# A memory-recurrent attention mixer with a gated MLP: GpSimd's left-over products wait for the second half's normalised scores, four half-tiles of MLP work change their step, and the last full projection moves ahead of three left-over groups

## The chip, the core and the metric

One core of a Trainium2 chip runs the whole kernel. Its engines are PE (TensorE, matrix products), DVE (VectorE), ACT (ScalarE), POOL (GpSimd) and SP (SyncE, which issues most transfers). The metric is the device time of one execution in microseconds. The kernel before takes 747.86 us in the median of 3 runs (747.28 to 749.27).

## The reference

The input `x` is 2048 rows of 512 numbers. Two branches read it and a gate mixes them:

```python
g = _sigmoid((x * gate_w).sum(-1, keepdims=True))
a = _A_ref(x, A_mem0, A_Wq, A_Wk, A_Wv, A_Wo, A_seg_len)
b = _B_ref(x, B_w1, B_b1, B_w2, B_b2)      # layernorm, 512 -> 1376, gelu, 1376 -> 512
return g * a + (1 - g) * b
```

Branch A is a recurrence over 64 segments of 32 rows. Each segment is joined to a memory of 8 rows, goes through attention with 32 heads of 128, and the first 8 rows of the result are the next segment's memory:

```python
for s in range(n_seg):
    h = jnp.concatenate([mem, xs], axis=1)           # 8 + 32 rows
    q, k, v = (jnp.einsum('btd,dhe->bhte', h, W) for W in (Wq, Wk, Wv))
    p = _softmax(jnp.where(mask, q @ k^T * scale, -1e9))
    o = jnp.einsum('bhte,hed->btd', p @ v, Wo)
    mem = o[:, :M, :]
```

## The kernel before, in words

The first 70 us run most of the MLP: the hidden layer of all 16 row tiles, and the second layer of seven of them. The hidden layers of the nine others (`DEF`, tiles 1, 3, 5, ...) go to DRAM and come back later. Then 63 steps, one a segment, do the recurrence, and an ending does segment 63. Instructions run on each engine in the order in which the code issues them (`tc.manual_schedule`), so the code is the schedule. `T, si = divmod(s, 4)` names the row tile and the segment in it.

A step has 40 rows, which do not fit the 32-row groups of PE. So 32 rows, 24 of the segment and the 8 of the memory, go through the step itself (`hT`), and the 8 left-over rows of each of four segments are projected together, a tile ahead, as "side" work (`left_qk`, `left_v`). On PE a step runs: queries and keys (L129), scores of the first half of the heads (`scores(s, 0)`), the values (L148), scores of the second half, the products with the values (`av`, L291 and L296, first half and then second), the output projection of the step before (`wo_pass`, L160, 32 matrix products of 512 columns into a bank `X`), and three transposing products that make the next memory (`new_mem`, L761, called with n = 0, 1, 2), whose casts (L763 on DVE) the next step's queries wait for. `run(n)` between these parts takes n pieces of side work.

What touches the change:

- **Normalising.** For the memory's queries the weights must be normalised before `av`. `mnorm(0)` does the first half of the heads and `mnorm(1)` the second: a reciprocal (L824) and a product on DVE that overwrites columns of `E` (L825, in the trace `E<-E,SbF` and `E<-E,RS`). The second half of `av` reads what `E<-E,RS` wrote. The 32 other queries are normalised a step later: DVE makes their reciprocals (L727, `R`), SP sends them to DRAM and back spread over all partitions (`r_dr`, then `Rb`), and GpSimd multiplies. That is `x_norm(s - 1)`, issued at the head of step s: two products into `UT` (L745, 128x384, for this step's `wo_pass`) and two into `UL` (128x128, the left-over rows, for `wo_left`, the side work of the next tile's step si = 2). Behind them GpSimd adds `R` into `racc` (L737), copies left-over queries (L250) and the next step's rows (L246). `Rb` has one buffer, so the next load of it waits for the last product that reads it.
- **Deferred MLP.** `mlp_halves` does the second layer of the nine deferred tiles in halves: one half is 4 matrix products of 256 columns into the bank `W` (L689), two halves use up one tile `hm` of the hidden layer, 11 of these a row tile. `next(mlp)` does one half. `hm_load` on SP fetches, once a step, in `recip_x`, as many tiles as were used up since (`owed`), into 5 buffers; step 2 also fetches four in one piece (`c`). After the eleventh, `mlp_out` writes the result (DVE `ct<-W`, 128x512, then a transfer). In step 2 the side work is `mlp_units(8)`: one unit is two halves.
- **Ending.** Segment 63 makes no memory. After its sums PE does three groups of `wo_left` (`run(3)`, 12 products from `UL`), then the `wo_pass` of segment 62, then `av`. `UL`'s last 8 columns are cleared by GpSimd just before (L896), behind the products of `x_norm(62)`.

## Time and profile before

| what | value |
|---|---|
| time, median of 3 runs (lowest to highest) | 747.86 us (747.28 to 749.27) |
| the profiled execution | 750.09 us, of which 748.2 us are the span from first to last instruction |
| PE busy | 732.8 us, 98% of the span |
| ACT, DVE, POOL busy | 536.7, 448.9 and 246.6 us |
| mean granted TensorE clock | 0.997 |

A step takes a little over 10 us, so step s = 31 lies at about 400 to 411 us. "Busy" of PE counts a product from its start to a modelled end; products overlap, so their starts tell more. A row of a timeline reads: start in us, us, engine, line, operation, output<-inputs, shape, count, and in brackets the idle time before it and what ended that. Several rows of one kind that follow each other are merged. In a row of a wait there stand the total, how many times, and the longest.

### The profile page before, as it was taken

Reading aid. Unit: us, or ns where it says so; the run is one execution under the profiler, and the core shown is the slowest. Engines: PE = TensorE matmul, PEld = TensorE weight load, DVE = VectorE, ACT = ScalarE, POOL = GpSimd, SP = SyncE. Lnnn points to the kernel's source line nnn. Section 1 sums busy time; section 2 is a strip of 40 time slices with the busy share of each in tenths; the row PEclk is TensorE's granted clock in tenths of the full one; section 3 lists DMA queues with packets and bytes.
Section 4 is the critical chain, followed back from the end, with each engine's and each line's share of the span. In section 5 each row is a group of like instructions: output and inputs, shape, how many; then the busy total and the mean of one; then the engine's idle time right before and its main releaser. Section 6 shows DMA issues by size and latency. Waiting matters only on the chain. (4 is left out here: it accounts for less than half of the span.)

```text
span 748.2 us, 44010 instructions
## 1 busy us (share of the span) xinstructions
PE 732.8 (98%) x19147; PEld 428.8 (57%) x19147; DVE 448.9 (60%) x1541; ACT 536.7 (72%) x1629; POOL 246.6 (33%) x515
## 2 busy tenths in 40 slices
PE   8999998999999999999999999999999999999997
PEld 5776554556565555555555555555555555555553
DVE  6877554656565555656565665556665656555554
ACT  6777765777777777777777777777777777777664
POOL 4001332332334333343234334243333343333331
PEclk9999999999999999999999999999999999999999
DMA  8999222222222323122321323231322313222221
GB/s 308 343 360 360 84 83 55 69 87 80 78 68 62 97 74 93 47 83 80 93 79 38 96 75 97 69 81 57 92 78 82 85 44 94 69 90 70 85 63 61
DMA packets 61944, 76.82 MB, mean 103 GB/s; under 512 B 26729, under 2 KB 51922, under 8 KB 60210
## 3 DMA queue, kind: packets, MB, share of 16 engines
q1 hardware_dynamic: 60802, 72.51, 31.1%
q8 instruction: 151, 2.47, 1.3%
q0 software_dynamic: 400, 0.92, 0.3%
q10 hardware_dynamic: 544, 0.52, 0.2%
q14 instruction: 47, 0.39, 0.2%
HBM read 60.21 MB, written 7.70 MB: 91 GB/s over the span
## 5 line engine op out<-in xcount | busy, mean ns | idle before, releaser
L134 ACT CAST Tb<-U 128x512 bf16<-128x512 f32 x288 | 168.8, 586 | 82.5 <-PE U L129 76.8
L745 POOL TENSOR_TENSOR UT<-XR,Rb 128x384 bf16<-128x384 bf16 x126 | 114.1, 927 | 324.6 <-DMA Rb<-r_dr 228.0
L129 PEld LDWEIGHTS <-hT 128*32 128x32 bf16 x4096 | 108.8, 97 | 97.8 <-issue 2.0
L129 PE MATMUL U<-Wq_sb,hT 128*32 128x512 bf16 x2048 | 145.9, 382 | 0.4 <-DVE hT L763 0.4
L129 PE MATMUL U<-Wk_sb,hT 128*32 128x512 bf16 x2048 | 145.2, 381 | 0.0
L148 PE MATMUL X<-Wv_sb,hT 128*32 128x512 bf16 x2048 | 142.9, 378 | 0.0
L160 PE MATMUL X<-Wo_sb,UT 128*32 128x512 bf16 x2016 | 120.8, 380 | 0.0
L834 ACT CAST V<-X 128x256 bf16<-128x256 f32 x256 | 88.7, 372 | 16.0 <-PE X L148 1.1
L138 DVE STREAM_TRANSPOSE QT<-Tb 128x256 f32<-128x256 f32 x128 | 57.0, 445 | 71.1 <-ACT Tb L134 70.9
L763 DVE CAST hT<-U 128x8 bf16<-128x8 f32 x126 | 20.8, 167 | 130.9 <-PE U L761 96.6
L160 PEld LDWEIGHTS <-UT 128*32 128x32 bf16 x2048 | 56.4, 96 | 55.7 <-issue 16.6
L721 ACT CAST XR<-U 128x256 bf16<-128x256 f32 x252 | 78.6, 438 | 0.0
L752 ACT CAST w<-X 128x128 bf16<-128x128 f32 x189 | 44.8, 310 | 41.7 <-PE X L160 41.0
L138 DVE STREAM_TRANSPOSE KT<-Tb 128x256 f32<-128x256 f32 x128 | 57.0, 445 | 25.9 <-ACT Tb L134 25.9
L737 POOL TENSOR_TENSOR racc<-racc,R 128x128 f32<-128x128 f32 x63 | 28.8, 457 | 105.7 <-DVE R L735 101.1
L148 PEld LDWEIGHTS <-hT 128*32 128x32 bf16 x2048 | 45.2, 95 | 20.6
L689 PE MATMUL W<-w_sb,hm 128*32 128x256 bf16 x728 | 50.5, 273 | 3.6 <-DMA hm<-h_dr 3.6
L865 ACT CAST UT<-U 128x64 bf16<-128x64 f32 x252 | 35.4, 227 | 25.9 <-PE U L296 25.9
L745 POOL TENSOR_TENSOR UL<-XR,Rb 128x128 bf16<-128x128 bf16 x126 | 51.5, 430 | 0.0
L809 ACT ACTIVATE E<-U 128x64 bf16<-128x64 f32 (+1 forms) x128 | 35.0, 273 | 9.3 <-PE U L271 0.4
L484 PEld LDWEIGHTS <-w_sb 128*128 128x128 bf16 (+1 forms) x352 | 34.1, 100 | 10.4
L160 PE MATMUL X<-Wo_sb,UL 128*32 128x512 bf16 x512 | 38.7, 379 | 1.0 <-POOL UL L896 1.0
(184 smaller groups left out, 1250.5 us busy)
## 6 DMA issues: line engine op xcount, KB each, us to landing
Rb<-r_dr SPq DMA_DIRECT2D x63, 512.0 KB, 3.9
Wv_sb<-in_A_Wv_dram SPq DMA_DIRECT2D x4, 1024.0 KB, 7.5
Wq_sb<-in_A_Wq_dram SPq DMA_DIRECT2D x4, 1024.0 KB, 8.5
Wk_sb<-in_A_Wk_dram SPq DMA_DIRECT2D x4, 1024.0 KB, 8.4
Wo_sb<-in_A_Wo_dram SPq DMA_DIRECT2D x4, 1024.0 KB, 12.6
VP<-VL SPq DMA_DIRECT2D x64, 64.0 KB, 3.7
hm<-h_dr SPq DMA_DIRECT2D x91, 32.0 KB, 2.6
c<-c_dr SPq DMA_DIRECT2D x16, 128.0 KB, 4.6
```

The source lines that it names most:

```text
L129: nc.tensor.matmul(bk[32 * j:32 * j + 32, :], lhsT=G[:, kc, :], rhs=W5[t][:, kc, h0:h1, j, :], start=(kc == 0), stop=(kc == KC - 1), tile_ ...
L134: nc.scalar.copy(out=Tb[:], in_=bk.rearrange("p (a b e) -> p a e b", a=8, b=2))
L138: nc.vector.transpose(out=dst[:, 8 * hf:8 * hf + 8, c0:c0 + 32, :].rearrange("p a r b -> p a (r b)").bitcast(FP32), in_=Tb[:].rearrange("p ...
L148: nc.tensor.matmul(bk[32 * j:32 * j + 32, :], lhsT=G[:, kc, :], rhs=Wv5[:, kc, 4 * vb:4 * vb + 4, j, :], start=(kc == 0), stop=(kc == KC - ...
L160: nc.tensor.matmul(bk[32 * c:32 * c + 32, :], lhsT=U_[:, j, i, :], rhs=Wo_sb[:, 4 * i + j, :], start=(n == 0), stop=(n == NW - 1), tile_po ...
L689: nc.tensor.matmul(W[32 * c:32 * c + 32, cc], lhsT=hm[:, 32 * c:32 * c + 32], rhs=w2_sb[:, fc, cc], start=(fc == 0 and h == 0), stop=(fc = ...
L721: nc.scalar.copy(out=XR[:, j], in_=U[j][:, 0:NG * 40].rearrange("p (i q) -> p i q", q=40)[:, :, 0:32])
L745: nc.gpsimd.tensor_tensor(out=out[:, :, 4 * h:4 * h + 4, o:o + b - a], in0=XR[:, :, 4 * h:4 * h + 4, a:b], in1=Rb[:, h, :, :, r:r + b - a] ...
L752: nc.scalar.copy(out=w[:, a:b], in_=bk[:, a:b])
L809: nc.scalar.activation(out=E[:, 4 * i2:4 * i2 + 4, c], in_=Sb[i2][:, :, c], func=ACTF.Exp, scale=scale)
L834: nc.scalar.copy(out=V[:, i0:i0 + 2, :].rearrange("p i e -> p (i e)"), in_=(X1, X2)[vb][:, 256 * h:256 * h + 256])
L865: nc.scalar.copy(out=UT[s % 2][:, j, :, 0:M], in_=U[j][:, 0:NG * 40].rearrange("p (i q) -> p i q", q=40)[:, :, 32:40])
```

## The change

Four edits, one of them in two places:

- `x_norm` takes a second argument: 0 makes the `UT` products, 1 the `UL` products. The first is still issued at the head of the step. The second is issued behind the value casts, after a new GpSimd copy of one column of `E` into a new tile `pend`. That copy reads a column that `mnorm(1)` writes, so GpSimd waits for it there. Only in the last segment do both stay at the head.
- `mlp_units(8)` of step 2 becomes `mlp_units(6)`: four halves fewer there. One half more is done at the end of step 3, three at the end of step 4.
- In the ending, `run(3)` comes behind `wo_pass` and not ahead of the reciprocal.

```diff
@@ side() @@
-            gens = [wo_left(T - 1, X1) if T >= 1 else mlp_units(8)]
+            gens = [wo_left(T - 1, X1) if T >= 1 else mlp_units(6)]
@@ x_norm @@
-    def x_norm(s):
+    def x_norm(s, l):
         T, si = divmod(s, SPT)
-        XR, Rb = XRs.pop(s), Rbs.pop(s)[:].rearrange("p (c j) (h q) -> p h j c q", c=4, h=2)
-        for out, o, a, b, r in ((UT[(s + 1) % 2], M, LEFT, 32, 0), (UL[T % 2], LEFT * si, 0, LEFT, 32 - LEFT)):
-            for h in range(2):
-                nc.gpsimd.tensor_tensor(...)
+        XR, Rb = XRs[s], Rbs[s][:].rearrange("p (c j) (h q) -> p h j c q", c=4, h=2)
+        out, o, a, b, r = ((UT[(s + 1) % 2], M, LEFT, 32, 0), (UL[T % 2], LEFT * si, 0, LEFT, 32 - LEFT))[l]
+        for h in range(2):
+            nc.gpsimd.tensor_tensor(...)
@@ head of a step @@
-            x_norm(s - 1)
+            x_norm(s - 1, 0)
+            if last:
+                x_norm(s - 1, 1)
@@ behind the value casts @@
+        if s:
+            nc.gpsimd.tensor_copy(out=pend[:], in_=E[:, NG - 1, 55:56])
+            x_norm(s - 1, 1)
         run(W1)
@@ end of a step @@
         for _ in fill:
             pass
+        for _ in range({SPT - 1: 1, SPT: 3}.get(s, 0)):
+            next(mlp, None)
+            mlp_outs()
@@ ending @@
     fill = wo_left(T, X2)
-    run(3)
     nc.vector.reciprocal(out=R[:, nx], in_=SbF[:, 0:32 * NG])
     nc.scalar.activation(out=rmin[:, nx], in_=R[:, nx], func=ACTF.Copy, accum_out=tot[:, 3:4])
     ws[s - 1] = wo_pass(UT[s % 2])
+    run(3)
```

In what follows, numbers behind a name tell buffers apart, and lines of the kernel after are a few higher (L865 is the copy into `pend`).

GpSimd, one step in the middle, before (what each row waits for stands in brackets):

```order
L246 COPY hT_86<-xT 128x4x24
L745 TENSOR_TENSOR UT_1372<-XR,Rb 128x4x4x24 [waits DMAHW3_49,Activation_49]
L745 TENSOR_TENSOR UT_1372<-XR,Rb 128x4x4x24
L745 TENSOR_TENSOR UL_1373<-XR,Rb 128x4x4x8 x2
L737 TENSOR_TENSOR racc<-racc,R 128x128 [waits DVE_49,Pool_49]
L250 COPY QT<-QL_89 128x16x8 [waits PE_49,Pool_49]
```

and after:

```order
L246 COPY hT_87<-xT 128x4x24
L746 TENSOR_TENSOR UT_1372<-XR,Rb 128x4x4x24 [waits DMAHW0_49,Activation_49]
L746 TENSOR_TENSOR UT_1372<-XR,Rb 128x4x4x24
L865 COPY pend<-E 128x1 [waits DVE_49,Pool_49]
L746 TENSOR_TENSOR UL_1374<-XR,Rb 128x4x4x8 x2
L738 TENSOR_TENSOR racc<-racc,R 128x128 [waits DVE_49,Pool_49]
```

The `UL` products now stand behind a copy that waits for DVE; nothing else of GpSimd's has moved.

DVE in the same part of a step, from the sums of the first half to the reciprocals, before:

```order
L823 TENSOR_REDUCE SbF<-U_119 128x32 [waits DVE_49,PE_49,Activation_49]
L824 RECIPROCAL SbF<-SbF 128x32 [waits DVE_49]
L825 TENSOR_TENSOR E<-E,SbF 128x4x16 [waits DVE_49]
L824 RECIPROCAL RS<-U_121 128x32 [waits PE_49]
L825 TENSOR_TENSOR E<-E,RS 128x4x16 [waits DVE_49,Activation_49]
L726 TENSOR_REDUCE SbF<-SbF 128x2x8 [waits PE_49]
```

and after:

```order
L829 TENSOR_REDUCE SbF<-U_119 128x32 [waits DVE_49,PE_49,Activation_49]
L830 RECIPROCAL SbF<-SbF 128x32 [waits DVE_49]
L831 TENSOR_TENSOR E<-E,SbF 128x4x16 [waits DVE_49,Pool_49]
L830 RECIPROCAL RS<-U_121 128x32 [waits PE_49]
L831 TENSOR_TENSOR E<-E,RS 128x4x16 [waits DVE_49,Activation_49]
L727 TENSOR_REDUCE SbF<-SbF 128x2x8 [waits PE_49]
```

The order is the same, but the first product now has two waits instead of one: it must not overwrite the buffer of `E` before the copy into `pend` of two steps ago has read it.

SP from the reciprocals of step 2 to the end of step 3, before:

```order
L730 DMA r_dr_78<-R 16x64
L661 DMA hm<-h_dr_69 128x128 x2
L661 DMA hm<-h_dr_70 128x128
L733 DMA Rb<-r_dr_78 128x1024
L674 DMA c_dr<-ct 128x512
L730 DMA r_dr_79<-R 16x64
L661 DMA hm<-h_dr_70 128x128 x4
L733 DMA Rb<-r_dr_79 128x1024
L189 DMA VP_94<-VL 128x1x256 x2
```

and after:

```order
L731 DMA r_dr_78<-R 16x64
L662 DMA hm<-h_dr_69 128x128 x2
L662 DMA hm<-h_dr_70 128x128
L734 DMA Rb<-r_dr_78 128x1024
L731 DMA r_dr_79<-R 16x64
L662 DMA hm<-h_dr_70 128x128 x2
L734 DMA Rb<-r_dr_79 128x1024
L675 DMA c_dr<-ct 128x512
L189 DMA VP_94<-VL 128x1x256 x2
```

Step 2 now uses up two tiles `hm` fewer, so step 3 fetches two and not four, and the result of row tile 1 leaves a step later.

More of the change, by code (lines that the diff above doesn't have):

```diff
@@ L615 @@
     good = lp.tile([P, 2], BF16)
+    pend = lp.tile([P, 1], BF16)
     bad = lp.tile([1, 1], I32)
@@ L738, in recip_x @@
         Rbs[s] = Rb
-    def x_norm(s):
+    def x_norm(s, l):
         T, si = divmod(s, SPT)
-        XR, Rb = XRs.pop(s), Rbs.pop(s)[:].rearrange("p (c j) (h q) -> p h j c q", c=4, h=2)
-        for out, o, a, b, r in ((UT[(s + 1) % 2], M, LEFT, 32, 0), (UL[T % 2], LEFT * si, 0, LEFT, 32 - LEFT)):
-            for h in range(2):
-                nc.gpsimd.tensor_tensor(out=out[:, :, 4 * h:4 * h + 4, o:o + b - a], in0=XR[:, :, 4 * h:4 * h + 4, a:b], in1=Rb[:, h, :, :, r:r + b - a], op=ALU.mult)
+        XR, Rb = XRs[s], Rbs[s][:].rearrange("p (c j) (h q) -> p h j c q", c=4, h=2)
+        out, o, a, b, r = ((UT[(s + 1) % 2], M, LEFT, 32, 0), (UL[T % 2], LEFT * si, 0, LEFT, 32 - LEFT))[l]
+        for h in range(2):
+            nc.gpsimd.tensor_tensor(out=out[:, :, 4 * h:4 * h + 4, o:o + b - a], in0=XR[:, :, 4 * h:4 * h + 4, a:b], in1=Rb[:, h, :, :, r:r + b - a], op=ALU.mult)
+        if l:
+            XRs.pop(s)
+            Rbs.pop(s)
     def wo_pass(U_, cuts=(0, Dm), bk=W):
```

## The prediction

> **What bounds the kernel now.** I read the page first, then the waits of PE, since the page leaves little else.

> ```profile
> PE 732.8 (98%) x19147; PEld 428.8 (57%) x19147; DVE 448.9 (60%) x1541; ACT 536.7 (72%) x1629; POOL 246.6 (33%) x515
> PE W L689 <- DMA hm<-h_dr: 3.6, 3, 2.4
> PE X L160 <- POOL UL L896: 1.0, 1, 1.0
> L825 DVE TENSOR_TENSOR E<-E,RS 128x64 bf16<-128x64 bf16 x63 | 17.8, 283 | 6.6
> ```

> PE is busy for 98% of the span, and the change neither adds nor removes a matrix product. So time can only come from moments in which PE stands still or runs slowly. The waits name two that the edits touch: 3.6 us for deferred MLP tiles, in three waits, and 1.0 us for the cleared `UL` in the ending. The last row belongs to the first edit: 63 second products of the normalisation at a mean of 283 ns.

> **Deferred MLP in steps 2 to 4.** The timeline of PE across the end of step 2 and through step 3:

> ```profile
> 103.81 0.19 PE L761 MATMUL U<-SelM,w 128*32 128x8 bf16 x4
> ...
> 105.90 0.39 PE L129 MATMUL U<-Wq_sb,hT 128*32 128x512 bf16 x4
> ...
> 111.64 0.61 PE L148 MATMUL X<-Wv_sb,GL 128*32 128x512 bf16 x8
> 112.07 0.29 PE L689 MATMUL W<-w_sb,hm 128*32 128x256 bf16 x4
> 112.18 0.20 PE L715 MATMUL SbF<-E,BO 128*32 128x40 bf16 x4
> ...
> 114.94 0.62 PE L148 MATMUL U<-Wv_sb,GL 128*32 128x512 bf16 x8
> 117.96 0.29 PE L689 MATMUL W<-w_sb,hm 128*32 128x256 bf16 x4 [2.41 <-DMA hm<-h_dr]
> ```

> Step 2: from the first memory product (103.81) to the next step's first query product (105.90) PE takes 2.09 us, because the four halves between the memory products need tiles that were fetched in the same step. These four go. How long the memory products take with nothing between them stands in the trace two steps before the ending, where the side work has run out:

> ```profile
> 719.17 0.36 PE L761 MATMUL U<-SelM,w 128*32 128x8 bf16 x8 [0.36 <-ACT w L752]
> ...
> 719.70 0.40 PE L129 MATMUL U<-Wq_sb,hT 128*32 128x512 bf16 x4
> ```

> That is 0.53 us (there the first also waited 0.36 us for its cast; in step 2 the five halves ahead of it stay and cover that). Gain: 2.09 - 0.53 = 1.56 us.

> Step 3: between eight value products and the next half lie 0.43 us where nothing waits (111.64 to 112.07), but 3.02 us at 114.94. The half at 117.96 asks for a tile that step 3 itself fetches, as all earlier ones were used up by then. After the change step 3 still has three tiles from step 2, uses two of them, and what step 4's end needs was fetched in step 3. Gain: 3.02 - 0.43 = 2.59 us.

> The clock: the windows view gives PE's granted clock in the stretch behind that wait, beside the same work of the step before.

> ```profile
> 105.90:109.60 3.70, 3.70 (x103) 1.92 (x96) 2.54 (x7) 1.78 (x4) 0.88 (x1) 1.00 0.53 164
> 119.10:122.50 3.40, 3.40 (x40) 1.38 (x36) 0.89 (x3) 1.35 (x3) 1.28 (x2) 0.51 0.48 143
> ```

> The columns are the window, its length, busy time of PE, PEld, DVE, ACT and POOL, the clock, the share of the DMA engines and GB/s. For 3.40 us after the 2.41 us wait the clock is 0.51: half of that is lost, 1.7 us. It is the only such stretch in the steps, and the only long wait, so I take the one for the other's consequence and expect it to go: 1.7 us. [...]

> The four halves come back, one in step 3 and three in step 4, at 0.11 us each (112.07 to 112.18): 0.43 us. Part could hide behind the casts that the next queries wait for; I take none. On SP, step 3 loses two fetches ahead of `Rb`, steps 4 and 5 have one more; each sits where SP waits for the store of `R` to land anyway. The result of row tile 1 is stored a step later and read eight steps later. Sum: 1.56 + 2.59 + 1.7 - 0.43 = 5.4 us gained; without the clock 3.7, with the halves hidden 5.8.

> **The left-over products.** A step in which they meet the second normalising product (first fence), and one in which they don't:

> ```profile
> 406.18 0.81 POOL L745 TENSOR_TENSOR UL<-XR,Rb 128x128 bf16<-128x128 bf16 x2
> ...
> 406.63 0.44 DVE L825 TENSOR_TENSOR E<-E,RS 128x64 bf16<-128x64 bf16 x1
> ...
> 406.77 0.27 PE L291 MATMUL U<-E,V 32*128 32x40 bf16 x16
> ...
> 407.12 0.28 PE L291 MATMUL U<-E,V 32*128 32x40 bf16 x16
> ...
> 407.83 0.40 PE L160 MATMUL X<-Wo_sb,UT 128*32 128x512 bf16 x4
> ```

> ```profile
> 446.89 0.37 DVE L824 RECIPROCAL SbF<-SbF 128x32 f32<-128x32 f32 x1
> 447.29 0.22 DVE L825 TENSOR_TENSOR E<-E,SbF 128x64 bf16<-128x64 bf16 x1
> 447.43 0.35 DVE L824 RECIPROCAL RS<-U 128x32 f32<-128x32 f32 x1
> 447.89 0.23 DVE L825 TENSOR_TENSOR E<-E,RS 128x64 bf16<-128x64 bf16 x1
> 448.03 0.27 PE L291 MATMUL U<-E,V 32*128 32x40 bf16 x16
> 448.17 0.35 PE L291 MATMUL U<-E,V 32*128 32x40 bf16 x16
> 448.94 0.61 PE L160 MATMUL X<-Wo_sb,UT 128*32 128x512 bf16 x8
> ```

> Beside GpSimd the product takes 0.44 instead of 0.23 us; it ends just behind GpSimd's, and the second half of `av` starts 0.05 us after it. From the first `av` to the projection pass 1.06 us instead of 0.91: of 0.21 us lost on DVE 0.15 reach PE, and 0.06 are made up behind. I count 15 such products, from

> ```profile
> 136.96 0.40 DVE L825 TENSOR_TENSOR E<-E,RS 128x64 bf16<-128x64 bf16 x1
> ...
> 705.52 0.44 DVE L825 TENSOR_TENSOR E<-E,RS 128x64 bf16<-128x64 bf16 x1
> ```

> the first to the last, together 2.3 us over 0.23. (All 63 are (283 - 226) x 63 = 3.6 us over; the rest stands behind the `UT` products, which stay where they are.) Moved behind the product, `UL` can't meet it: 2.3 - 15 x 0.06 = 1.4 us gained, at most 2.3.

> But the edit adds a wait: the first product must now also wait for the copy into `pend`, two steps old and long done. A second wait is an extra event on DVE's queue, and the trace shows what that does: the first product, with one wait, starts 0.03 us behind its reciprocal (446.89 + 0.37 to 447.29); the second, with two, 0.11 us (447.43 + 0.35 to 447.89). So the first should start 0.07 to 0.08 us later, in 60 steps. The second reciprocal follows the first product by 0.14 us, so the second product moves too, and the step at 447 has no slack: its `av` starts the same 0.05 us behind the product as the delayed one. If the made-up 0.06 us holds here too, 0.01 us a step is left: 0.6 us. Bounds: 0, and 60 x 0.07 = 4.2 us. I take 0.7, since the delayed step is the nearest row.

> What GpSimd now does later costs nothing:

> ```profile
> POOL racc L737 <- DVE R L735: 101.1, 62, 4.2
> L727 DVE RECIPROCAL R<-SbF x63: 557/557/560, 79.6 to 726.6; 128x64 f32<-128x64 f32 x63
> 410.46 0.17 DVE L763 CAST hT<-U 128x8 bf16<-128x8 f32 x1 [1.97 <-PE U L761]
> DMA to landing us min/median/max: 1.7/1.8/3.5
> ```

> Behind the copy stand `UL` (0.81 us), `racc` and two copies for the next step; GpSimd waits 101.1 / 62 = 1.6 us a step ahead of `racc`, which covers `UL` and a copy of a few tenths (not in the trace: no POOL row is that small; between 0 and the 0.46 us of `racc`). `UL` then runs to about 408.2 beside DVE's reciprocal and copies; were these held up by all of 0.81 us, the memory casts still have 1.97 us idle ahead of them. The next load of `Rb` waits for `UL`, but also for the store of `R` (407.83 + 1.8), later than 408.2. Net of this edit: 1.4 - 0.7 = 0.7 us gained, from 2.3 gained to 2.8 lost.

> **The ending.**

> ```profile
> 734.87 1.80 POOL L745 TENSOR_TENSOR UT<-XR,Rb 128x384 bf16<-128x384 bf16 x2 [6.66 <-DMA Rb<-r_dr]
> ...
> 737.74 0.83 PE L160 MATMUL X<-Wo_sb,UL 128*32 128x512 bf16 x12 [0.96 <-POOL UL L896]
> ...
> 738.66 0.22 DVE L906 TENSOR_TENSOR E<-E,R 128x64 bf16<-128x64 bf16 x1
> ...
> 740.23 0.27 PE L291 MATMUL U<-E,V 32*128 32x40 bf16 x16
> ```

> `wo_pass` needs the `UT` products, done at 736.67, and not the clearing of `UL`. It starts at about 736.7 instead of waiting to 737.74, and covers that clearing. `av` moves from 740.23 to 739.2; its weights are ready at 738.9, so the move is real, and everything behind it shifts. Gain 1.0 us, at most the 0.96 of the wait and some hundredths, at least 0.7 if `av` then waits.

> **Sum.** 5.4 + 0.7 + 1.0 = 7.1 us. The profiled execution becomes 750.09 - 7.1 = 743.0; the median stands 2.2 below it, and the same gain from the median gives 747.86 - 7.1 = 740.8.

> **The rivals.**
> - *The added wait is not made up.* For: `av` has no slack. Against: delays of up to 0.06 us vanished. It costs 3.5 us more: 744.3.
> - *The slow clock stays*: the stretch has another cause than the wait. For: nothing but its place ties it to the wait. Against: no other stretch like it in the steps. 740.8 + 1.7 = 742.5. [...]
> - *The wait for a tile moves to step 3's or 4's end.* The tile would have to land later than half a step after its fetch. One wait of 2.4 us: 743.2.
> - *Slower: `UL` holds up the reciprocals `R`.* They now run beside `UL` in each step. If each came 0.8 us later, so would `Rb` and the next step's `UT` products, which then run into the second normalising product: the step at 406, whose `UT` products end 0.45 us ahead of it (406.18 to 406.63), would be one, and by my count 25 of 62 would be, at some 0.5 us each, 13 us, and 7.1 gained become 6 lost: 754. It decides from a delay of about 0.7 us. Against: none of the 63 reciprocals took longer than 560 ns, though before the change a late `UL` lay beside some of them.

> **How the numbers follow.** Chances: forecast 0.70, wait not made up 0.14, clock stays 0.05, tile wait moves 0.04, `R` held up 0.05, nothing measurable 0.02. A measurement here can tell about 0.3%, 2.2 us, from no change. Faster: 0.70 + 0.14 + 0.05 + 0.04 = 0.93; same 0.02; slower 0.05. The range reaches up to the rival at 744.3 and down to 738.5: 2.3 gained by the left-over products with no loss and the halves hidden make 9.1, 738.8, and a few tenths of spread between runs.

> **What would show it.** Waits of PE: no row of `hm`; none of `UL` in the ending. A clock of 1.00 through the steps. A mean of `E<-E,RS` near 245 ns, no `UL` beside it. `E<-E,SbF` starting 0.1 us behind its reciprocal; the projection still 0.91 us behind the first `av`, or 0.98 if the wait is not made up. I am wrong if that distance grows in all steps, or if `R` lasts longer than 0.56 us.

## The result, and the profile after

The changed kernel takes 744.62 us (median; 742.35 to 747.07), the kernel before in the same comparison 747.86 us (745.35 to 750.3). The ratio is 0.9963, with a 95% interval of 0.9945 to 0.9981: 2.8 us faster (1.4 to 4.1). The forecast was 740.8 with a range of 738.5 to 744.3, a gain of 7.1. The direction was right, the gain less than half, the time 0.3 us outside the range. In a second comparison the ratio was 0.9982 (0.9967 to 0.9996), or 1.3 us.

The waits of PE after, the longest two and the first one of the normalising products (columns: total, times, longest):

```profile
PE U L528 <- POOL ident masks.py:199: 1.5, 1, 1.5
PE X L461 <- DVE y L454: 0.7, 1, 0.7
...
PE U L291 <- DVE E L831: 0.4, 2, 0.2
```

No row for `hm` is left, and none for `UL` in the ending. The timeline of PE, at the end of step 2, at the end of step 3, in one step in the middle and in the ending:

```profile
103.31 0.36 PE L765 MATMUL U<-SelM,w 128*32 128x8 bf16 x8
103.76 0.22 PE L765 MATMUL SbF<-SelM,w 128*32 128x8 bf16 x8
103.87 0.40 PE L129 MATMUL U<-Wq_sb,hT 128*32 128x512 bf16 x4
...
113.68 0.29 PE L690 MATMUL W<-w_sb,hm 128*32 128x256 bf16 x4
113.80 0.19 PE L765 MATMUL U<-SelM,w 128*32 128x8 bf16 x4
...
401.64 0.27 PE L291 MATMUL U<-E,V 32*128 32x40 bf16 x16
...
401.85 0.28 PE L291 MATMUL U<-E,V 32*128 32x40 bf16 x16
...
402.56 1.91 PE L160 MATMUL X<-Wo_sb,UT 128*32 128x512 bf16 x32
...
732.09 1.91 PE L160 MATMUL W<-Wo_sb,UT 128*32 128x512 bf16 x32
733.82 0.83 PE L160 MATMUL X<-Wo_sb,UL 128*32 128x512 bf16 x12
734.59 0.27 PE L291 MATMUL U<-E,V 32*128 32x40 bf16 x16
```

The memory products of step 2 take 0.56 us to the next query product (103.31 to 103.87; 2.09 before, 0.53 forecast). In step 3 the half starts without a wait. The windows view at the place of the slow stretch shows the full clock:

```profile
119.10:122.50 3.40, 3.40 (x136) 2.08 (x135) 2.76 (x11) 2.78 (x13) 1.47 (x5) 1.00 0.44 39
```

In the middle step the projection starts 0.92 us behind the first `av` (401.64 to 402.56). DVE in the same step, and the group of all second products:

```profile
400.98 0.22 DVE L831 TENSOR_TENSOR E<-E,SbF 128x64 bf16<-128x64 bf16 x1
401.12 0.35 DVE L830 RECIPROCAL RS<-U 128x32 f32<-128x32 f32 x1
401.57 0.23 DVE L831 TENSOR_TENSOR E<-E,RS 128x64 bf16<-128x64 bf16 x1
```

```profile
L831 DVE TENSOR_TENSOR E<-E,RS 128x64 bf16<-128x64 bf16 x63 | 15.7, 249 | 6.6
```

The second products have a mean of 249 ns, forecast near 245, 283 before. So far everything is as forecast. What the forecast doesn't have is at the very end. The last DMA issue and the span, before:

```profile
core 0 of [0], span 748.2 us
...
744.88 0.82 SPq L943 DMA_DIRECT2D out_dram<-o x2
```

and after:

```profile
core 0 of [0], span 744.3 us
...
739.25 0.82 SPq L955 DMA_DIRECT2D out_dram<-o x2
```

From the last issue to the end pass 3.3 us before and 5.1 us after, with the same work in between.

To see where the rest went, each profiled execution is cut at the first `av` of steps 2, 5, 60 and 63 (in us; the last column counts DVE's records in the trace ahead of the branch that closes the program, waits that became instructions of their own included). All kernels of the experiments below but one stand in it, so that edits can be compared over several executions:

| kernel (edits it has) | start to 2 | 2 to 5 | 5 to 60 | 60 to 63 | 63 to end | span | DVE |
|---|---|---|---|---|---|---|---|
| before | 100.05 | 37.06 | 568.63 | 34.50 | 8.01 | 748.24 | 2028 |
| after (units, products, ending) | 99.81 | 31.76 | 569.80 | 33.22 | 9.74 | 744.33 | 2088 |
| before, again | 101.06 | 35.98 | 571.13 | 33.37 | 8.01 | 749.54 | 2028 |
| after, again | 99.50 | 32.17 | 568.72 | 33.53 | 9.59 | 743.49 | 2088 |
| units alone | 99.72 | 31.90 | 570.27 | 35.15 | 8.01 | 745.05 | 2028 |
| products alone | 100.05 | 34.06 | 570.12 | 34.65 | 9.58 | 748.46 | 2088 |
| ending alone | 100.02 | 34.62 | 568.46 | 33.48 | 8.17 | 744.76 | 2028 |
| units, ending | 100.09 | 32.63 | 570.50 | 33.67 | 8.01 | 744.90 | 2028 |
| before + 60 clears | 99.93 | 33.02 | 569.30 | 33.35 | 9.54 | 745.13 | 2088 |
| the same, again | 100.35 | 36.36 | 568.47 | 33.99 | 9.61 | 748.79 | 2088 |
| after + 68 clears | 101.00 | 31.58 | 569.38 | 33.28 | 8.09 | 743.33 | 2156 |
| products behind `racc` | 99.93 | 31.85 | 568.88 | 33.80 | 8.10 | 742.56 | 2028 |
| the same, again | 99.43 | 32.75 | 569.10 | 33.35 | 8.23 | 742.86 | 2028 |
| the same + 60 clears | 99.93 | 32.33 | 568.11 | 33.34 | 9.71 | 743.42 | 2088 |
| the same + 128 clears | 104.75 | 31.93 | 569.12 | 33.49 | 8.02 | 747.30 | 2156 |

Two things stand out. The last stretch has two values, 8.0 to 8.2 and 9.5 to 9.7, and DVE's count decides which. And the stretch from 2 to 5 of the kernels that still have the old units is anything from 33.0 to 37.1: the profile from which the forecast was made has the longest.

### The profile page after: what moved, and what is told of

Its sections match the earlier page's. It is cut to its first block, busy times and chain, and to the rows that moved or that the text cites. A ratio compares the mean times of both kernels' runs of the same rounds, so it can differ in the third digit from the quotient of the medians.

```text
span 744.3 us, 44193 instructions
## 1 busy us (share of the span) xinstructions
PE 732.0 (98%) x19147; PEld 429.6 (58%) x19147; DVE 454.8 (61%) x1541; ACT 536.6 (72%) x1629; POOL 257.1 (35%) x577
## 3 DMA queue, kind: packets, MB, share of 16 engines
q8 instruction: 151, 2.47, 1.4%
## 4 chain that ended last, share of the span: by engine, by line
PE 95%; DMA 2%; DVE 1%; ACT 1%; issue 1%; DVEq 0%
PE U L129 34%; PE X L160 19%; PE X L148 17%; PE X L129 4%; PE U L291 3%; PE W L690 3%; PE U L484 2%; PE U L148 2%; PE U L267 2%; PE U L491 2%; DMA xt<-in_A_x_dram 2%; PE SbF L484 1%; PE W L484 1%; PE SbF L267 1%; PE U L296 1%
## 5 line engine op out<-in xcount | busy, mean ns | idle before, releaser
L129 PEld LDWEIGHTS <-hT 128*32 128x32 bf16 x4096 | 109.3, 97 | 95.1 <-DVE hT L767 0.6
L129 PE MATMUL U<-Wq_sb,hT 128*32 128x512 bf16 x2048 | 145.0, 380 | 0.0
L129 PE MATMUL U<-Wk_sb,hT 128*32 128x512 bf16 x2048 | 144.6, 379 | 0.0
L148 PE MATMUL X<-Wv_sb,hT 128*32 128x512 bf16 x2048 | 143.9, 378 | 0.4 <-issue 0.4
L160 PE MATMUL X<-Wo_sb,UT 128*32 128x512 bf16 x2016 | 120.7, 380 | 0.0
L160 PEld LDWEIGHTS <-UT 128*32 128x32 bf16 x2048 | 56.3, 96 | 56.5 <-issue 19.2
L148 PEld LDWEIGHTS <-hT 128*32 128x32 bf16 x2048 | 45.7, 95 | 21.9 <-issue 1.4
L129 PE MATMUL U<-Wk_sb,GL 128*32 128x512 bf16 x496 | 39.3, 377 | 0.0
L160 PE MATMUL X<-Wo_sb,UL 128*32 128x512 bf16 x512 | 38.9, 380 | 0.0
```

Of the source, the lines that this page charges most:

```text
L129: nc.tensor.matmul(bk[32 * j:32 * j + 32, :], lhsT=G[:, kc, :], rhs=W5[t][:, kc, h0:h1, j, :], start=(kc == 0), stop=(kc == KC - 1), tile_ ...
L148: nc.tensor.matmul(bk[32 * j:32 * j + 32, :], lhsT=G[:, kc, :], rhs=Wv5[:, kc, 4 * vb:4 * vb + 4, j, :], start=(kc == 0), stop=(kc == KC - ...
L160: nc.tensor.matmul(bk[32 * c:32 * c + 32, :], lhsT=U_[:, j, i, :], rhs=Wo_sb[:, 4 * i + j, :], start=(n == 0), stop=(n == NW - 1), tile_po ...
```

## The experiments

The theory after the first comparison of traces: the 60 events that the copy into `pend` adds to DVE's queue cost time in the steps and, by their number, at the closing branch. Rivals: the moved units give their gain back later; or the differences are chance.

### Each edit alone

The units alone (`mlp_units(6)` and the halves at the ends of steps 3 and 4):

> Only the deferred units move; the products and the ending stay as before. Theory (the loss sits in the extra events on DVE's queue, which this kernel does not have): the stretch from step 2's first `av` to step 5's becomes 5.3 us shorter, as in the changed kernel, no wait for `hm`, the clock 1.00; steps 5 to 60 and the last 8.0 us behind the last `av` stay as before; the span becomes 748.2 - 5.3 = 742.9. Rival (the moved units give time back later, by their stores and fetches): steps 5 to 60 become about 1 us longer, the span 744. Rival (the end of the program differs by chance): its last part may be 8.0 or 9.7 us.

Ratio 0.9961 (0.9937 to 0.9985). No wait for `hm`, 31.90 us from 2 to 5, 8.01 at the end. That the stretch 5 to 60 is 1.6 us longer, as the rival has it, stands against the same stretch of the kernel before repeated, which is 2.5 us longer: it is spread. So the edit gains 2.9 us in the times (1.1 to 4.7 by the interval), where the forecast had 5.4.

The products alone (`x_norm` in two parts and the copy into `pend`):

> Only the left-over products move, with the copy into `pend`. Theory (extra events on DVE's queue): steps 5 to 60 become 1.2 us longer as in the changed kernel, the first product starts 0.10 us behind its reciprocal, steps 12, 25 and 38 lose about 0.25 us each, and from the last `av` to the end 9.7 us pass instead of 8.0; the span becomes 748.2 + 1.2 + 1.7 = about 751, slower. The forecast on record: 0.7 us faster, 747.5. Rival (the loss in the steps came from the moved units): steps 5 to 60 stay within 0.3 us of before. Rival (the end differs by chance): 8.0 us at the end.

Ratio 1.0001 (0.9977 to 1.0025): no gain, where the forecast had 0.7. The end is 9.58 us, as the theory had it. The stretch 5 to 60 is 1.5 us longer than before, which is within the spread just named. The span, 748.5, stayed below the expected 751, and this kernel showed the first surprise: it has the old units, and yet its stretch from 2 to 5 is 3.0 us shorter than before.

The ending alone:

```diff
-    run(3)
     nc.vector.reciprocal(out=R[:, nx], in_=SbF[:, 0:32 * NG])
     ...
     ws[s - 1] = wo_pass(UT[s % 2])
+    run(3)
```

> Only the ending is reordered. Theory: no wait for `UL`, and the last `av` comes 0 to 1.4 us earlier, by what that wait is in the execution of before; about 0.7 us on the mean of the profiles so far (1.0, 1.4, 0.5, 0); 8.0 us from the last `av` to the end. Forecast on record: 1.0 us. Rival (the pass waits for its own tiles instead): nothing gained.

Ratio 0.9992 (0.9972 to 1.0012), too small to tell from nothing by the times. The wait for `UL` is gone, and the stretch 60 to 63 is 33.5 us; the other executions with this edit have 33.2 to 33.8.

Units and ending, without the products:

> The changed kernel without the edit of the products: units and ending alone. Theory: no wait for `hm`, no wait for `UL` in the ending, 8.0 us at the end; 3.1 us (units) and 0.7 us (ending) gained, a ratio of 0.995, somewhat below the changed kernel's, since the products' edit with its 60 events loses 1.6 us at the end and gains at most that in the steps. Forecast on record for these two edits: 6.4 us, a ratio of 0.9914. Rival (the edit of the products is worth its price): a ratio above the changed kernel's.

Ratio 0.9931 (0.9906 to 0.9955), better than both comparisons of the changed kernel (0.9963 and 0.9982). This points to the products' edit costing more than it brings, by little: the medians are 744.14 against 744.62 and 745.61, the kernel before ran slower beside this one (749.37), and the interval overlaps the first of the two. The forecast's 6.4 us for the two, 0.9914, lies inside the interval, but 2 to 5 in the profile is 32.63 here, and the sum by the means of the table (below) is 3.8.

### How long PE waits for the deferred tiles

> The kernel before once more, for a second profile. Theory (how long PE waits for a deferred tile differs from execution to execution, and the profile that the forecast was made from was an unlucky one): the waits for `hm` in steps 2 and 3 come out elsewhere than 3.6 us in all, likely between 1 and 3 us, and if none is above 2 us the clock stays 1.00; the stretch from step 2's first `av` to step 5's is then 1 to 4 us shorter than in the first profile. The wait for `UL` in the ending lies anywhere between 0 and 1.4 us. From the last `av` to the end 8.0 us. Rival (the kernels with a longer DVE queue changed these waits): 3.6 us again, 2.4 in step 3, the clock at half behind it.

The second profile of the kernel before has a wait of 2.28 us in step 3, two waits of 3.0 us together, 1.1 us less from 2 to 5, and no wait for `UL` in the ending at all:

```profile
117.90 0.29 PE L689 MATMUL W<-w_sb,hm 128*32 128x256 bf16 x4 [2.28 <-DMA hm<-h_dr]
```

```profile
119.00:122.50 3.50, 3.50 (x40) 1.39 (x36) 1.17 (x4) 1.48 (x3) 0.72 (x1) 0.54 0.60 187
```

The same half in the other kernels that have the old units, and the clock behind it. Ending alone:

```profile
116.89 0.29 PE L689 MATMUL W<-w_sb,hm 128*32 128x256 bf16 x4 [2.08 <-DMA hm<-h_dr]
```

```profile
119.00:122.50 3.50, 3.50 (x112) 1.97 (x104) 2.04 (x5) 2.73 (x6) 1.81 (x3) 1.00 0.45 123
```

Products alone:

```profile
116.35 0.29 PE L690 MATMUL W<-w_sb,hm 128*32 128x256 bf16 x4 [1.90 <-DMA hm<-h_dr]
```

The kernel before with 60 clears, twice (the clears are the subject of the next part); first execution:

```profile
115.30 0.29 PE L692 MATMUL W<-w_sb,hm 128*32 128x256 bf16 x4 [0.40 <-DMA hm<-h_dr]
```

and the second, with its clock:

```profile
117.58 0.29 PE L692 MATMUL W<-w_sb,hm 128*32 128x256 bf16 x4 [2.19 <-DMA hm<-h_dr]
```

```profile
119.00:122.50 3.50, 3.50 (x44) 1.42 (x40) 0.80 (x3) 1.17 (x2) 2.12 (x3) 0.59 0.40 114
```

So this wait was 2.41, 2.28, 2.19, 2.08, 1.90 and 0.40 us in six executions in which PE has the same work and SP the same fetches at this place. Behind the first three the clock falls to about half (0.51, 0.54, 0.59), behind the others it stays at 1.00. Ordered by all that PE waits for `hm`, 3.6, 3.2, 3.0, 2.9, 2.6 and 1.2 us, the stretch from 2 to 5 reads 37.06, 36.36, 35.98, 34.62, 34.06 and 33.02. Their mean is 35.2; the nine executions with the new units have 31.6 to 32.8, mean 32.1. The edit's worth is the difference, 3.1 us, and between 0.9 and 5.0 against a single execution. The waits and the clock make up the whole range: less all waits for `hm`, and less 1.7 us where the clock fell, the six read 31.3 to 31.8.

How often the clock falls can be read from all executions, since the mean clock of each is on record and not only that of the profiled ones. In 70 executions with the new units it is 0.998 or more. In 87 of the kernel before, run beside the experiments, it is 0.996 or 0.997 in 17, 0.998 in 8 and higher in 62; the 17 take 749.0 us on the mean, the 62 take 747.4. So the slow stretch comes in about a fifth to a quarter of the executions (17 to 25 of 87), and these take 1.6 us longer, near the 1.7 that the forecast gave to it. On the mean of all it is worth some 0.4 us.

To see whether the clock follows the wait, the tiles were fetched later:

```diff
         nc.sync.dma_start(r_dr[s % 2][:], R[0:P:8, 8 * NG:RW])
+        nc.sync.dma_start(Rb[:]..., r_dr[s % 2][:]...)
         hm_load(owed[0])
         owed[0] = 0
-        nc.sync.dma_start(Rb[:]..., r_dr[s % 2][:]...)
```

> The kernel before with the deferred tiles fetched behind `Rb` instead of ahead of it, so that they land about 2 us later: PE's wait in step 3 becomes 3 to 5 us, and that in step 2 one of 2 to 3 us. Theory (a wait of more than some 2.2 us is followed by a stretch at about half clock): a stretch of some 3.4 us at 0.5 behind each wait above 2.2 us; the span 4 to 8 us longer than before. Rival (the slow stretch has another cause): a clock of 1.00 behind at least one wait longer than 2.4 us.

The two waits of that kernel, and the windows behind them:

```profile
106.39 0.40 PE L689 MATMUL W<-w_sb,hm 128*32 128x256 bf16 x8 [3.15 <-DMA hm<-h_dr]
...
122.23 0.41 PE L689 MATMUL W<-w_sb,hm 128*32 128x256 bf16 x4 [3.97 <-DMA hm<-h_dr]
```

```profile
106.70:110.10 3.40, 3.40 (x56) 1.43 (x52) 1.50 (x5) 0.59 (x1) 2.29 (x4) 0.54 0.13 43
...
122.60:126.00 3.40, 3.40 (x56) 1.24 (x48) 0.75 (x4) 0.80 (x2) 2.18 (x4) 0.50 0.07 19
```

Both waits, 3.15 us (2 to 3 expected) and 3.97, are followed by about half the clock, also in step 2, where no other kernel has a slow stretch. The ratio is 1.0124 (1.0093 to 1.0156), about 9 us slower, more than the 4 to 8 expected. Here the wait causes the slow clock.

But it is not the length of the wait alone that decides. In all sixteen traces the granted clock changes only at multiples of 3.41 us, counted from its first change (in the kernel before at 6.37, 119.01, 122.43 and 747.07 us, that is 33, 1 and 183 such lengths apart). Cut at these places, the kernel before and the one with the ending alone read as follows around the wait (first the 2.41 us, then the 2.08 us; PE's busy time stands behind the length, the clock third from the end):

```profile
115.60:119.01 3.41, 1.05 (x36) 0.67 (x40) 0.46 (x4) 0.99 (x4) 0.00 (x0) 1.00 0.39 97
119.01:122.42 3.41, 3.41 (x40) 1.37 (x32) 0.98 (x4) 1.36 (x3) 1.20 (x2) 0.50 0.48 148
```

```profile
112.68:116.09 3.41, 2.12 (x40) 0.96 (x32) 0.87 (x4) 2.29 (x8) 1.31 (x4) 1.00 0.14 30
116.09:119.50 3.41, 2.61 (x64) 1.42 (x68) 0.72 (x5) 1.17 (x2) 0.00 (x0) 1.00 0.57 156
```

The 2.41 us lie almost wholly in one window, which leaves PE busy for 1.05 us of it, and the next window has half the clock. The 2.08 us are split over two, 1.29 and 0.80, and nothing follows. Over all windows of the sixteen traces, one at full clock with PE busy for 1.41 us or less is always followed by one at half clock, and one with 1.80 us or more never. So in these traces it depends on where a wait of about 2 us falls whether it slows the clock, and that differs from execution to execution. The wait of 3.97 us brought two windows at half clock, 6.83 us, of which the first began while PE still waited.

### The end of the program

What follows the last DMA issue is the branch (L966 before, L978 after) by which all engines skip the general case. In the trace's records DVE's branch stands at 745.75 before, and DVE's next instruction comes 0.60 us later; after, the branch is at 740.10 and the next instruction comes 3.13 us later, while SP waits for DVE. To tell DVE's count from the edits, clears of one element were put on DVE in the MLP of the first 90 us; with 60 of them the kernel before has as many DVE instructions as the changed kernel:

```diff
             a_mm(blk, fc)
+            if 16 <= n < 76:
+                nc.vector.memset(pad[:], 0.0)
```

> The kernel before, with 60 clears of one element on DVE added in the first 90 us, where DVE has idle time: DVE's queue gets as long as in the changed kernel, with no wait added and nothing moved. Theory (where DVE's instructions lie in the stream that is fetched sets the time of the closing branch): from the last `av` to the end 9.7 us instead of 8.0, and small stalls of DVE in steps other than before, the same ones as in the changed kernel; the span about 750. Rival (the end is longer because of what the changed kernel does there, or by chance): 8.0 us, the span 748.2.

```profile
core 0 of [0], span 745.1 us
...
740.24 0.82 SPq L946 DMA_DIRECT2D out_dram<-o x2
```

From the last issue to the end 4.9 us, 2.93 of them at the branch: 60 more instructions ahead of the branch make the end longer, and no edit of the change is needed for it. The time, though, was not longer (ratio 0.9988, 0.9967 to 1.0009). With clears in the changed kernel (called 68; the code makes 69, and one wait event falls away), 128 instructions more than in the kernel before:

> [...] Theory (the place of the closing branch within a fetch sets its time): from the last `av` to the end 8.0 us again, though the queue is longer still; the span 1.6 us below the changed kernel's. Rival (a longer queue as such makes the end longer): 9.7 us or more.

```profile
core 0 of [0], span 743.3 us
...
739.88 0.82 SPq L958 DMA_DIRECT2D out_dram<-o x2
```

3.4 us, and 0.58 at the branch; ratio 0.995 (0.9932 to 0.9968), although PE waits 0.8 us for a clear in the head. No run before this one had shown that 128 instructions more bring the short end back. The changed kernel once more:

> The changed kernel once more. Theory (the closing branch on DVE is set by where its instructions lie): from the last `av` to the end 9.7 us again, and the stalls of DVE in steps 12, 25 and 38 again; no wait for `hm`. Steps 5 to 60 may differ by up to 1 us either way. Rival (chance): 8.0 us at the end, the stalls in other steps.

9.59 us at the end, 2.97 at the branch. Over all sixteen profiles of this study, DVE's next instruction comes 0.60 us behind the branch with 2028 records ahead of it (eight profiles), 0.58 with 2156 (two), and 2.93 to 3.13 with 2088 (six). So it isn't the length of the queue but where its instructions lie. The stalls of DVE came again too: in steps 12, 25 and 38 the projection starts 1.15 to 1.19 us behind the first `av`, 0.92 in the median, in all three executions with the copy and 2088 records; with 68 instructions more ahead none of the three steps is that long.

Such stalls lie 128 records apart, or a multiple of it. From its record 350 on, in the first steps, DVE starts an instruction 0.16 to 0.37 us later than the others of its kind, without a wait that explains it, 39 times in the sixteen traces, and each time its record, counted from 0, has the number 63 above a multiple of 128 (575, 831, 959, 1599 and others; in the first profile of the changed kernel 575, 959, 1343, 1727 and 1855, late by 0.25, 0.37, 0.25, 0.19 and 0.16 us). In the steps 12, 25 and 38 just named, the records 575, 959 and 1343 are instructions of the normalisation. The branch at 2028 and the one at 2156 stand 45 records behind such a place, the one at 2088 stands 105 behind it. The page of the profile (before) lists two queues of instructions:

```profile
q8 instruction: 151, 2.47, 1.3%
...
q14 instruction: 47, 0.39, 0.2%
```

q14 brings instructions in packets of 0.39 MB / 47 = 8.3 KB, q8 in packets of 2.47 MB / 151 = 16.4 KB. Of the 44010 instructions that the page counts, 38294 are PE's (19147 products and as many weight loads), 254 for each packet of q8, and some 5700 the other engines', 122 for each packet of q14. Which queue serves which engine the page doesn't say; if q8 serves PE and q14 the others, a packet of q14 holds some 122 instructions, an estimate from these counts, and not far from the 128 between the stalls. With 128 more ahead of it, the branch took 0.58 us against 0.60. That the branch goes to instructions which DVE does not hold yet, and that the 3 us are their fetch, is the author's conjecture; no run shows it.

### Whether the end is in the times

The kernel before with 60 clears once more, and the kernel of the next part with 60 and with 128 clears:

> The kernel before with 60 clears once more, with more executions. Theory: 9.6 us from the last `av` to the end again, the wait for the deferred tile of step 3 back at 1.9 to 2.4 us (in the first profile it was 0.4, by chance), and a time 0 to 3 us above the kernel before. Rival (the clears make the deferred tiles land earlier, and so pay for the end): a wait of 0.4 us again, and a time no higher than that of the kernel before.

> The kernel with the products behind `racc`, with 60 more clears of one element on DVE in the first 90 us: DVE's queue as long as in the changed kernel, and no deferred tile awaited that could blur the comparison. Theory (the place of the closing branch costs 1.6 us in every execution): 9.6 us from the last `av` to the end, and a median 1.6 us above that of the kernel with 128 clears. Rival (the price shows in the profiles only, or is made up elsewhere, as the times of the kernel before with 60 clears suggest): the two medians agree within 0.5 us.

> [...] Theory: 8.0 to 8.2 us from the last `av` to the end; up to 1 us lost in the head, where PE waits for the clears as it did in the changed kernel with 68 of them; a ratio of about 0.994 to 0.995. Rival (a longer queue as such costs): slower than with 60 clears.

The first kernel now has the wait of 2.19 us, 9.61 us at the end and a ratio of 1.0012 (0.9991 to 1.0033): the short waits of its first profile were a draw. Its two ratios together, 0.9988 and 1.0012, are no change, where 1.6 us would be 1.0021, so they don't show the loss. With 60 clears the kernel of the next part has 9.71 us at the end and a ratio of 0.995 (0.993 to 0.997); without them its ratios are 0.9943 and 0.9926, 0.5 and 1.8 us better, which agrees with 1.6 but is no proof. With 128 the end is 8.02, but the clears cost 4.7 us in the head, so that its time (ratio 1.0009) decides nothing; 748.63 less 4.7 would be 0.5 us below the kernel with 60. What is sure is that the time contains the end: in all sixteen profiled executions it is 1.8 us more than the span, with either end. The 1.6 us are thus measured in every profile, while the medians are mixed: the kernel before with 60 clears speaks against a loss, the changed kernel with clears (0.995 against 0.9963 and 0.9982) for one.

### The products without the copy

The left-over products need a place behind DVE's second product. `racc` waits for DVE's copies into `R` anyway, so they can stand behind it and need no wait of their own:

```diff
-        Rb = cw.tile([P, 16, 8 * NG], FP32, tag="Rb", bufs=1, name="Rb")
         nc.sync.dma_start(r_dr[s % 2][:], R[0:P:8, 8 * NG:RW])
         ...
-        nc.sync.dma_start(Rb[:]..., r_dr[s % 2][:]...)
         ...
+        nc.gpsimd.tensor_tensor(out=racc[:, 0:RW], ...)
+        if s:
+            x_norm(s - 1, 1)
+        Rb = cw.tile([P, 16, 8 * NG], FP32, tag="Rb", bufs=1, name="Rb")
+        nc.sync.dma_start(Rb[:]..., r_dr[s % 2][:]...)
         mask_put(0)
-        nc.gpsimd.tensor_tensor(out=racc[:, 0:RW], ...)
...
-        if s:
-            nc.gpsimd.tensor_copy(out=pend[:], in_=E[:, NG - 1, 55:56])
-            x_norm(s - 1, 1)
```

> As the changed kernel, but the left-over products stand behind the sum `racc`, which waits for DVE's copies into `R` anyway; no copy into `pend`, and DVE's queue is as long as before. Theory (extra events): the first product starts 0.03 us behind its reciprocal again, steps 5 to 60 gain the 1.4 us of the collisions against before, the last part is 8.0 us; the span becomes 748.2 - 5.3 - 1.4 - 1.0 - 0.2 = about 740.3, 4 us below the changed kernel. Rival (the loss comes from elsewhere, chance or the moved units): the span stays near 743 to 744. Rival (the products run so late that the next `Rb` waits for them): the `UT` products start later and meet DVE's second product in more steps; slower than the changed kernel.

> The kernel with the products behind `racc` once more, with more executions. Theory (the edit's gain is there, and the added events took it away): from the first `av` to the projection 0.94 to 0.95 us on the mean of steps 5 to 59, as in its first profile, where the kernels with the products unmoved have 0.964 to 0.981 and those with the added wait 0.969 to 1.008; 8.0 us at the end; a ratio of about 0.994 to 0.995. Rival (the first profile was a lucky draw): 0.97 again.

Ratios 0.9943 (0.9922 to 0.9963) and 0.9926 (0.99 to 0.9952), medians 744.02 and 743.41: on a par with units and ending alone, and ahead of the changed kernel. The first product starts 0.03 us behind its reciprocal again. From the first `av` to the projection the mean of steps 5 to 59 is 0.942 and 0.959 us, and 0.961 and 0.966 with the clears, against 0.964 to 0.999 in the executions with the products unmoved: on the better side, but not the 0.94 to 0.95 that was expected of all. The expected span of 740.3 was missed by 2.3 us in the first and 2.6 in the second. Of these, 1.7 and 1.9 us lie in steps 5 to 60, for which 1.4 us had been taken off an execution on the short side (568.63, where seven executions with unmoved products have a mean of 569.5).

The second products of the second execution, from the groups of DVE:

```profile
L832 DVE TENSOR_TENSOR E<-E,RS 128x64 bf16<-128x64 bf16 x63 | 18.2, 289 | 6.6
```

289 ns (265 in the first), although no `UL` product lies beside them any more: the 12 that overlap GpSimd's products at all lie beside `UT` products.

## Why the prediction was wrong, and where it was right

By the table's means the changed kernel gains 3.1 (2 to 5: 35.2 to 32.1), 0.7 (60 to 63: 34.2 in six executions without the ending's edit, 33.5 in nine with it) and nothing in steps 5 to 60 (569.5 with the products unmoved, seven executions, and 569.5 with the copy, four), and loses 1.6 at the end (8.1 with 2028 or 2156 records, 9.6 with 2088). That is 2.2 us, and both comparisons, 2.8 and 1.3, agree with it. Against the forecast's 7.1, term by term:

- **Deferred MLP, 5.4 forecast, 3.1 measured.** The mechanism was right in each part, and against the profile used even the size (37.06 to 31.76 is 5.3). The failed step is "Gain: 3.02 - 0.43 = 2.59 us" with the 1.7 us of clock behind it: it took a wait for a DMA from one execution for the wait of all. The one used was the longest of six, and it slowed the clock, which three of the six did not; over all executions of the kernel before, no more than a quarter or so have the slow stretch, so that this term is some 0.4 us on the mean and not 1.7. The warning stood in the forecast itself: the execution was 2.2 us above the median, and yet "the same gain from the median" was subtracted. A gain that is made of such waits shrinks when counted from a better execution. (Nor is this execution alone: 14 of the 16 profiled ones are above the median of their kernel's runs, so the stretches in the table lean to the long side.)
- **The clock.** Taking the wait for its cause was right; that it comes in every execution was not. A wait of 2.19 us sufficed, where all of it lay in one window of 3.41 us, and one of 2.08 us split over two did not.
- **The left-over products, 0.7 forecast, 0.0 in the steps.** The price of the added wait was right: the first product starts 0.10 us behind its reciprocal (median of all steps 0.104, 0.034 before), and the median from `av` to the projection went from 0.909 to 0.920 us, 0.01 a step. So the rival "not made up" did not happen, though its 744.3 is near the time. `UL` never meets the second product now, and the mean fell (249 and 268 ns in the two executions, 281 to 330 in those with the products unmoved). But its 1.4 us do not show: on the stretch 5 to 60, which spreads over 2.7 us, a term of that size needs more executions than these. The version without the copy has 568.8 there (four executions), 0.7 below, which would leave the copy's price at the 0.7 of the forecast, but the spread is too wide to show that.
- **The ending, 1.0 forecast, 0.7 measured.** `wo_pass` starts without the wait and `av` follows, as forecast. The wait for `UL` was again one draw: 1.0 in the profile used, between none (twice) and 1.4 in the others.
- **The end of the program, not forecast, 1.6 lost in the profiles.** The step that failed is "A second wait is an extra event on DVE's queue": it was priced by what it delays, 60 times, and not as 60 more instructions that shift all behind them. No row of the profile before could have shown the price; the branch and DVE's count could have been a rival.
- **`R` held up, and a moved tile wait**, did not occur: no reciprocal `R` took longer than 560 ns, and no `hm` row is left.

What stays open: what makes a deferred tile land early or late; whether the 3 us at the branch are the fetch that its place suggests; and why the times of the kernel before with 60 clears don't show them.

## What to carry to other kernels

A wait for a DMA in one profile is a draw: before its removal is counted at its full length, see whether that execution lies above the median of the runs, and price the wait by several executions. A wait that is spared can also spare the slow clock behind it, but only in the executions that have it (here about 1.6 us, in 17 to 25 of 87): the mean clock of all runs tells how many. And count the instructions that an edit adds to an engine's queue, events too: where they move a branch, the end of the program can change by more than the edit (here 60 wait events, and an end longer by 1.6 us in the profiles).
